# v pooled over four tokens by one load and three adding transfers, with new orders of instructions

## The chip, the cores and the metric

The kernel runs on one core of a Trainium2 chip. The metric is the device time of one execution in microseconds (us). The core has five engines that each take their instructions in order: TensorE (PE) for matmuls and transposes, VectorE (DVE), ScalarE (ACT) and GpSimd (POOL) for work on vectors, SyncE (SP) that here only issues transfers. A transfer (DMA) is issued by an engine and carried out by 16 DMA engines; who needs its data waits for a semaphore that it raises when it has landed.

## The reference

Inputs are q, k and v (4 batches, 8 heads, 576 tokens, 64 numbers each) and five weight arrays. For each batch:

```
q_d, k_d, v_d = means of q, k, v over groups of 4 tokens      # 144 tokens
coarse = softmax(q_d k_d^T / 8) v_d, each row repeated 4 times
local  = softmax(q k^T / 8 over |i - j| < 4) v
x      = coarse + local                                       # 576 x 512, heads side by side
u      = x + Re(fft over tokens and over the 512 features of x)
x      = u + relu(layernorm(u) @ w_ch1) @ w_ch2               # 512 -> 2048 -> 512
gate   = sigmoid(causal convolution of x with 5 taps per feature)
out    = (gate * (x @ w_val)) @ w_out
```

The change concerns v_d, which the coarse attention multiplies from the right.

## The kernel before, in words

Features or keys lie on the 128 partitions, tokens along the free dimension. Large matmuls split each float32 operand in two float16 parts, high and low, and add the products (the tiles hh and hl, u, W, FH and FL). Work comes in 4 batches; the part after the attention runs in 3 units of 192 tokens per batch, 12 in all. Batch 0 has code of its own for its attention (lines 1600 to 1830), which fills the first 60 us or so together with the preparation of the weights; the attention and the transform of batches 1 to 3 are interleaved with the MLP and the gated part of the batch before, whose matmuls (lines 1319, 1340, 1389, 1494, 1510) are the bulk of PE's work.

In batches 1 to 3 the function `dense` makes the list of steps of the local attention and of what it loads, and `lowres` that of the coarse one. The coarse part takes the pooled q and k from a tile qkT, computes the scores of a head on PE (sc, line 957), the exponentials E on ACT, transposes them (eT, line 992; copied to ET by ACT) and multiplies them by the pooled v (po, line 1002). Pooled v is the tile `vr`, 72 partitions (keys) x 2 (halves of the keys) x 512 (heads and numbers), in float32. It is a sum over the four tokens, the division by 4 standing in the copy to ET.

How vr comes about before: v lies in DRAM as `v_p` with the four tokens of a group apart (indices: batch, half of the keys kc, token r of the group, key, head and number). `pool_v4(n)`, n from 0 to 3, loads a quarter of it (half of the keys, four of the eight heads) in two transfers of 72 x 2 x 256 into two tiles v, and `pooled_v` adds them: `ptv` = tokens 0 + 1, `vr` = tokens 2 + 3, `vr` = vr + ptv. GpSimd does all three (the helper `add` with engine G, line 528). So a batch takes 8 loads of 144 KB, issued by SP, and 12 additions by GpSimd; three batches take 24 and 36. The tiles v are in the ring `pr` of two slots, ptv in the ring `E` of three, and vr in the ring `M` of two, which kT (k of the dense part) uses too. Batch 0 makes its pooled v on PE (line 1761) and isn't touched.

The order in which each engine takes its instructions is written out by hand in the table `ORDER`: one text for each engine, of numbers `part.index`, a part being a step of the program and the index the place of an instruction among those that the part gives to that engine. A loop at the end (line 2061) ties the instructions in that order; semaphores for the data come on top. Which slot of a ring a tile takes is written in the table `SLOT`. Nothing moves by itself when a step gets shorter: an engine goes on with the next instruction of its row as soon as that one's waits are met.

Other names that follow: `dP` are the weights of the local attention, scaled by 1/sum on GpSimd for some groups (helper at line 525); `vw` is v by windows for the local attention; `uc` and `sq` are the sums of x over the features and of its squares, for the layernorm; `r` is 1/sqrt of the variance by Newton steps on GpSimd (lines 1178 and 1184), which DVE and then ACT turn into the normalised `u`; `sx` and `sums`/`so` are weights on their way to float16 through DRAM; `fs` a sum for the transform; `s_` and `iv_` are scales (powers of two) and their inverses, from `p2a` and `p2b` (lines 573 to 577).

Of the kernel before, what the change touches and what calls it, by code (L numbers as in the profile page):

```python
# [14 lines left out]
ALU = mybir.AluOpType  # L15
# [5 lines left out]
QC = SD // 2  # L21
# [22 lines left out]
    "prp.E": "0120120101202102120120120120120121021201201201220210210210210210210210120102102102100201201201201201201201210210210",  # L44
# [6 lines left out]
    "prp.pr": "010101010101010101010110101010010101",  # L51
# [15 lines left out]
225.0-2 195.2 237.1 237.0 237.2 238.1 238.0 225.3 238.2 267.1 267.0 275 277 280.1 280.0 282 283.1 283.0 285.0 294.1-3  # L67
291.0-1 294.4 291.2 298.0 291.3-8 326.1 286.0 298.1 298.3 298.2 286.1 285.1 326.0 347.0 121 347.1-3 403.0 333.1 333.0
367.1 367.0 345 367.2 368.0-1 369 368.2 370.1 403.1 433 315 370.0 370.2 403.2-3 408 412 424 419 423 427 444 450.1
450.0 430.1 430.0 499.0 488.1 488.0 467 499.1 488.2 491.1 491.0 492.1 491.2 492.0 492.2 499.2-3 493.1 493.0 493.2  # L70
546.0-1 539 535 546.2-3 545.0 550.1 550.0 545.1 553 554 559.1 559.0 609 639
""",
    "vector": """
0 30 20 18 21 32 25.1 25.0 28 41.1 41.0 48.0 27 38 48.1 23 48.2 54 65.0 31 58.0 34 65.1 42 59 71 77.1 77.0 75 58.1 60
85 55 56 63 68 73 52 81.0 86 81.1-3 140 67 81.4 70.0-1 70.3 70.2 83 130 129 132 107 81.5 109 110 113.1 113.0 114 117
118 125 81.6 79 143 84 169.3 88 136 137 139 133 167.0 145 146 147 150 153 131.0 154 156 157 159 165 163 192.1 167.1
160 169.0 192.0 169.1 169.4 164 167.2 209 168.0-1 131.1 192.2 193.0 168.2 192.3 192.5 192.4 131.2 170.0 169.2 169.5
170.1-2 210 186 187 172.0 197.1 197.0 247.0 171.0 211 171.1-2 172.3 172.1 172.4 212 193.1 172.5 172.2 174.0-1 227
247.1-2 193.2 247.3 174.2 197.2-3 228 197.4 224.0-1 253.0 197.5 173 247.4 229 258 247.5-6 188 259 253.1 239.0 239.3
232 189 239.4 239.1 255.2 230 239.5 239.2 255.0-1 255.3 265 224.2-3 225 234 233 241 249.3 249.0 253.2 269 224.5 224.4  # L80
253.3-5 292.0 236 292.1 274 257.0 257.3 253.6-7 292.2 249.1 249.4 278 243 249.5 249.2 253.8-10 302.0 246 253.11 292.3
257.1-2 261.0 253.12 302.2 253.13 261.1 257.4-5 263.3 263.0 299.0 302.1 253.14 293.0 284 407.0 302.3 251 292.4-5 288
263.1-2 263.4 261.2 303.3 303.1 261.3 263.5 303.2 267.1 304.1 293.1 293.3 304.2-3 300 293.4 303.0 261.5 261.4 293.2
267.0 299.1 305 293.5 295 271.0 310 273.0 271.2 271.1 273.2 273.1 261.6 271.3 314 275.1 299.2 273.3 275.0 323 306.1
296.0 277.1 277.0 275.2 277.2 327 299.3-4 335 296.1 280.0 306.2 280.1 282.0 407.1 296.2 407.2 296.3-4 283.0 304.0
296.5 282.1 283.1 306.3 297.0-1 306.0 309 407.4 285 297.3-5 286 291.0-1 338 291.2 342 297.2 291.3 294.0 291.4 322
326.1 326.0 294.1-2 350.1 313.0 326.2 291.5 339 291.6 326.3 313.1 333.1 333.0 298.0 311.0 354 350.0 298.2 298.1 357
311.1 364 407.3 328.3 328.1 328.0 328.2 329.1-2 329.0 331.2 331.1 329.3 332 334.2 334.1 371 331.3 331.0 334.0 334.3
341.0 319 341.1 379 347.0 324 344 347.1-2 345.0-1 355.0 333.2 356.0 333.3 347.3-4 388 355.2 359.0 462.1 366 355.1
347.5-6 356.2 359.2 347.7 345.2 355.3 356.1 345.3 356.3 347.8 395 376.0 376.3 347.9 400 359.3 359.1 378.0-2 347.10  # L90
361.1 378.3 361.0 406.1 361.3 406.0 378.4 376.1-2 376.4 361.2 413 381.0 372.0 376.5 372.1 410 377.0 387.0 381.3 377.1
387.1-3 414.0-1 462.0 383.0 381.4-5 381.1-2 429 462.2 383.1 387.4 383.2 420 538.0 417.0 414.3 385.0 414.2 385.3 417.3
417.1-2 421.3 393.2 385.1-2 383.3 421.1 421.0 538.1 426.0 385.4-5 394.0-3 383.5 426.3 426.1 390.0 390.3 393.3 394.4
390.1 421.2 445 390.2 426.2 434 390.4-5 432 383.6 393.0 397.0-1 383.4 397.2 403.0 397.3 393.1 399.0 399.2 404.0 399.1
404.2 403.1 404.1 403.2 399.3 448 451 408.1 408.0 404.3 403.3 438 412.0-1 408.2 403.4 412.2 403.5-8 419.0 403.9 419.1
455.0 403.10 397.4 446.0 424.0 423.0 439.0 459 446.1 455.1 538.2 424.1 423.1 457 439.1 402.0-3 427.0 427.2 427.1 402.4
460.2 460.1 465 463.2 460.3 473 427.3 466.2 409.0 430.0 471 430.2 430.1 463.1 409.1 430.3 409.2 452.0 409.3 444.0
463.3 452.1 444.1 409.4 466.3 460.0 452.2 474 442 478 452.3 538.4 452.4 415.0 463.0 415.1-2 466.1 469.3 444.2 452.5
415.3 444.3 452.6 450.1 450.0 452.7 415.4 452.8-10 581 452.11-14 452.17 482 422.0 452.18 452.15 484 422.1-3 469.2
469.1 466.0 469.0 422.4 450.2-3 452.16 476.0 479.0 467.0-1 452.19 441 479.1 476.1 467.2-3 489.1 489.0 497.2 496.0-3  # L100
496.5 496.4 496.6 497.1 502.3 502.0 499.0 443 519 502.4-5 502.1-2 504.2 504.1 499.1 508.0 508.3 509.0 499.2 509.1
497.3 497.0 499.3 508.1-2 504.0 508.4-5 538.3 509.2-3 509.5 511.0 499.4 511.1 504.3 509.6 509.4 513.3 513.0 506.2
# [12 lines left out]
624.5 609.13 609.12 616.3 624.4 624.6 616.2 616.0 629.0-2 629.5 609.14-15 623.0 629.6 629.3-4 639.0 633.1 626.0 637.0
# [369 lines left out]
def attn_moe_kernel(ctx, tc, q_t, k_t, v_p, v_w, w1, w2, w_val, conv_t, w_out, c_feat, c_seq, c_band, c_eye, c_plm, out):  # L485
# [261 lines left out]
    def attn_steps(b):  # L747
# [37 lines left out]
        def dense():  # L785
# [1337 lines left out]
```

## Time and profile before

| | |
|---|---|
| median of 3 runs | 656.34 us (656.07 to 657.16) |
| profiled execution, its own time | 656.75 us |
| its span, first to last instruction | 654.7 us |
| mean granted clock of TensorE | 0.989 |
| busy: PE, DVE, ACT, POOL | 644.5, 527.3, 355.3, 103.5 us |
| busy share of the 16 DMA engines, hardware queue | 39.8% |

The profile was taken of one execution. An engine's busy time counts its work, not the issue of transfers or waits on semaphores. The views used below are the page's totals; windows, that is, busy time in stretches of the span; an engine's waits, with what released it; groups of instructions by line; the timeline, where equal instructions that follow each other are one row with a count (x2) and the time from the first one's start to the last one's end; the issues of DMAs; and the chain of waits, followed back from the last instruction. A buffer's number is left out of its name, so W is any of the weight buffers. A releaser is inferred from semaphores.

### The profile page before, as it was taken

Reading aid. Unit: us, or ns where it says so; the run is one execution under the profiler, and the core shown is the slowest. Engines: PE = TensorE matmul, PEld = TensorE weight load, DVE = VectorE, ACT = ScalarE, POOL = GpSimd, SP = SyncE. Lnnn points to the kernel's source line nnn. Section 1 sums busy time; section 2 is a strip of 40 time slices with the busy share of each in tenths; the row PEclk is TensorE's granted clock in tenths of the full one; section 3 lists DMA queues with packets and bytes.
Section 4 is the critical chain, followed back from the end, with each engine's and each line's share of the span. In section 5 each row is a group of like instructions: output and inputs, shape, how many; then the busy total and the mean of one; then the engine's idle time right before and its main releaser. Section 6 shows DMA issues by size and latency. Waiting matters only on the chain.

```text
span 654.7 us, 20391 instructions
## 1 busy us (share of the span) xinstructions
PE 644.5 (98%) x8626; PEld 574.5 (88%) x8627; DVE 527.3 (81%) x1138; ACT 355.3 (54%) x1057; POOL 103.5 (16%) x162
## 2 busy tenths in 40 slices
PE   9989999999999999999999999999999999999997
PEld 4668899999998887998988888997899989998995
DVE  3999989989988876789999969996778787587554
ACT  2787659788644656677444778644232332414223
POOL 0000121310121703510310153032010100100000
PEclk9959999999999999999999999999999999999999
DMA  9994583023343012332482363352524234343201
GB/s 313 393 339 165 210 309 117 20 85 138 108 126 129 2 37 69 102 115 90 137 288 82 116 215 117 112 177 77 180 85 163 98 112 133 113 146 130 99 3 48
DMA packets 44301, 89.96 MB, mean 137 GB/s; under 512 B 3391, under 2 KB 24895, under 8 KB 43186
## 3 DMA queue, kind: packets, MB, share of 16 engines
q1 hardware_dynamic: 44210, 88.67, 39.8%
q8 instruction: 67, 1.10, 0.7%
q14 instruction: 24, 0.20, 0.1%
HBM read 73.77 MB, written 16.65 MB: 138 GB/s over the span
## 4 chain that ended last, share of the span: by engine, by line
PE 85%; DVE 7%; DMA 3%; ACT 2%; POOL 1%; issue 1%; SPq 0%; ACTq 0%; DVEq 0%; POOLq 0%
PE pc L1389 25%; PE ph L1319 11%; PE ph L1340 8%; PE out L1510 7%; PE val L1494 6%; PE p L1340 6%; DVE W L522 3%; PE ab L1070 2%; PE pc L1294 1%; PE po L1761 1%; PE dO L879 1%; PE po L1604 1%; DMA raw<-in_moe_w_ch_dram 1%; PE st L1154 1%; PE sc L957 1%; PE po L1002 1%
## 5 line engine op out<-in xcount | busy, mean ns | idle before, releaser
L1389 PE MATMUL pc<-hh,W 128*128 128x192 f16 x1232 | 169.8, 246 | 0.0
L1389 PEld LDWEIGHTS <-W 128*128 128x128 f16 x1848 | 152.7, 98 | 4.0 <-issue 1.6
L1389 PE MATMUL pc<-hl,W 128*128 128x192 f16 x616 | 129.3, 246 | 0.0
L1319 PE MATMUL ph<-u,W 128*128 128x192 f16 x960 | 94.5, 246 | 0.6 <-ACT u L1199 0.6
L1319 PEld LDWEIGHTS <-W 128*128 128x128 f16 x960 | 80.2, 98 | 2.8 <-issue 1.4
L1340 PEld LDWEIGHTS <-W 128*128 128x128 f16 x1632 | 79.0, 98 | 2.7 <-issue 0.8
L522 DVE SCALAR_TENSOR_TENSOR W<-X,cw,W 128x192 f32<-128x192 f32 x160 | 62.5, 426 | 9.1 <-ACT W L1457 8.8
L1340 PE MATMUL ph<-u,W 128*128 128x96 f16 x960 | 65.1, 206 | 0.2
L1352 ACT ACTIVATE hh<-r 128x384 f16<-128x384 f32 x48 | 24.3, 519 | 71.9 <-DVE r L528 60.2
L1494 PE MATMUL val<-yy,W 128*128 128x192 f16 x576 | 59.1, 246 | 0.1
L1494 PEld LDWEIGHTS <-W 128*128 128x128 f16 x576 | 47.6, 98 | 2.0 <-issue 0.9
L1340 PE MATMUL p<-u,W 128*128 128x96 f16 x672 | 47.9, 206 | 0.0
L1510 PE MATMUL out<-W,gh 128*128 128x512 f16 x144 | 45.8, 379 | 0.0
L528 DVE TENSOR_TENSOR r<-ph,r 128x384 f32<-128x384 f32 (+1 forms) x48 | 21.8, 454 | 21.0 <-PE ph L1340 19.2
L843 ACT ACTIVATE dP<-dS,dmx 128x64 f32<-128x64 f32 x120 | 36.5, 331 | 0.4
L522 DVE SCALAR_TENSOR_TENSOR hl<-r,hh 128x384 f16<-128x384 f32 x48 | 26.2, 564 | 9.4 <-ACT hh L1352 8.9
L528 DVE TENSOR_TENSOR r<-p,r 128x192 f32<-128x192 f32 (+1 forms) x72 | 28.2, 419 | 5.5 <-PE p L1340 3.1
L1323 ACT ACTIVATE hh<-ph 128x384 f16<-128x384 f32 x40 | 19.4, 490 | 19.5 <-PE ph L1319 17.6
L522 DVE SCALAR_TENSOR_TENSOR W<-W,W 128x1024 int32<-128x1024 int32 x24 | 28.9, 1220 | 0.2
L1510 PE MATMUL out<-W,gl 128*128 128x512 f16 x72 | 27.3, 379 | 0.0
L843 ACT ACTIVATION_READ_ACCUMULATOR dP<-dS,dmx 128x1 f32 x120 | 26.9, 224 | 0.0
L1510 PEld LDWEIGHTS <-gh 128*128 128x128 f16 x144 | 14.1, 98 | 13.6
(308 smaller groups left out, 1429.5 us busy)
## 6 DMA issues: line engine op xcount, KB each, us to landing
W<-sums SPq DMA_DIRECT2D x32, 512.0 KB, 4.4
W<-in_moe_w_ch_dram SPq DMA_DIRECT2D x12, 1024.0 KB, 6.9
sm<-sums SPq DMA_DIRECT2D x16, 512.0 KB, 6.7
out_dram<-osb SPq DMA_DIRECT2D x17, 256.0 KB, 4.1
vw<-in_vw_dram SPq DMA_DIRECT2D x8, 512.0 KB, 4.8
w1f<-W SPq DMA_DIRECT2D x8, 512.0 KB, 3.1
sums<-so SPq DMA_DIRECT2D x16, 256.0 KB, 2.9
v<-in_vp_dram SPq DMA_DIRECT2D x24, 144.0 KB
```

The source lines that it names most:

```text
L522: return eng.scalar_tensor_tensor(out=out, in0=in0, scalar=scalar, in1=in1, op0=op0, op1=op1)
L528: return eng.tensor_tensor(out=out, in0=a, in1=b, op=ALU.add)
L843: A.activation(out=s_[:, z, a], in_=pss[par][:, z, a], func=AF.Exp, scale=SCALE, bias=mx[:, par, z, a:a + 1], accum_out=su[:, par, z, a:a ...
L879: T.matmul(out=pos[x][par * 64:par * 64 + 64, a2, o:o + nq], lhsT=vw[g][row, 2 * z + hf, c:c + D], rhs=pts[z][row, par, a2, hf * 64:hf * 6 ...
L1070: T.matmul(out=ps[0:n, c0:c1], lhsT=d[x][:, c, sd, e, n0:n0 + n], rhs=feat[:, w, c, c0:c1], start=(t == 0), stop=(t == 5),)
L1319: T.matmul(out=ps[:, e], lhsT=w1_ap(pw, kc, 2 * g + e), rhs=uh[px][:, kc, :], start=(t == 0), stop=(t == 11))
L1323: A.activation(out=h_, in_=ps, func=AF.Relu)
L1340: T.matmul(out=out[:, e * HT:e * HT + HT], lhsT=w(pw, kc, e), rhs=b_[x](px, kc), start=(kc, pw, px) == (0, 0, 0), stop=(kc, pw, px) == (1, ...
L1352: A.activation(out=h[0], in_=x, func=AF.Relu)
L1389: T.matmul(out=ps[m // 2][:, m % 2], lhsT=w2_ap(pw, kk, m), rhs=x[px][:, e], start=(kk == 0 and (pw, px) == (0, 0) and m % 2 == 0), stop=( ...
L1494: T.matmul(out=ps[:, e], lhsT=wv_ap(pw, kc, 2 * mh + e), rhs=m_["y"][px][:, kc, :], start=(t == 0), stop=(t == 11))
L1510: T.matmul(out=ps, lhsT=(gh, gl)[px][:, kc, t * 128:(t + 1) * 128], rhs=wo_ap(pw, kc), start=(n == 0), stop=(n == 11))
```

## The change

`pool_v4` gets another meaning. Its argument is now r, one of the four tokens of a group. For r = 0, SP loads a 72 x 2 x 512 slice, 288 KB, straight into vr. For r = 1, 2 and 3, GpSimd issues a transfer of the same shape into the same place, with `accum_op=ALU.add`, which adds to what is there. Each of these has to wait until the one before has landed. `pooled_v` is not called any more; the tiles v and ptv are gone, and with them the slots of ring `pr` in `SLOT` and some of ring `E`. A batch has 1 load and 3 adding transfers in place of 8 loads and 12 additions. Step times and all other code stay; since the parts of the program have other instructions, the numbers in `ORDER` are written anew for all five engines, and other instructions are moved by that too. PE does the same matmuls as before.

```diff
@@ -895,13 +891,15 @@
                 steps.append((0.1, lambda z=z: [load_k(z, 0, KW), load_q(z, 0, S)]))
             steps.append((0.1, lambda: [load_vw(g) for g in range(3)]))
 
-            def pool_v4(n):
-                x = [pr_t("v4", [QC, 512]) for _ in range(2)]
-                kc, h = n // 2, n % 2
-                for r in range(2):
-                    load(out=x[r].rearrange("p (r c) -> p r c", r=2),
-                         in_=v_p[b, kc, 2 * r:2 * r + 2, :, h * 256:h * 256 + 256].rearrange("r g c -> g r c"))
-                pooled_v([(kc, x)], n, h * 4, 4)
+            def pool_v4(r):
+                if r == 0:
+                    new_vr()
+                x = v_p[b, :, r, :, :].rearrange("k g c -> g k c")
+                o = d["vr"].rearrange("p k h d -> p k (h d)")
+                if r == 0:
+                    load(out=o, in_=x)
+                else:
+                    nc.gpsimd.dma_start(out=o, in_=x, accum_op=ALU.add)
             v1 = [(0.1, lambda n=n: pool_v4(n)) for n in range(4)]
             for z in range(2):
                 for w in range(1 if b == 1 else 2):
```

In the tables:

```diff
-    "prp.E": "0120120101202102120120120120120120121021201201201220210210210210210210210120102102102100201201201201201201201210210210",
+    "prp.E": "0120120101200201201201201201210212012012011021021021021021021012010210210211201201201201201201210210210",
...
-    "prp.pr": "010101010101010101010110101010010101",
...
     "gpsimd": """
-0.0 5.1 5.0 136.1 136.0 137.0 139.1 139.0 137.1 183.0-2 195.1 195.0 193.0-1 0.1 294.0 193.2-8 183.3 219.1 219.0 219.2
...
+5.0 0.1 0.0 5.1 136 137 139.1 139.0 219 183 193 237 225.0-1 225.3 225.2 238 267.1 267.0 275 277 315 280 282.1 283.1
```

Code before the changed function has moved up by four lines in the changed file and code behind it by two, so that line 528 is now 524, 1002 now 1000, and 1184 now 1182.

GpSimd's row in the third batch. Before, from the second of two multiplications of dP on, with ten of the batch's twelve additions behind it:

```order
L525 TENSOR_TENSOR dP_3463<-dP_3463,dsu 128x512
L528 TENSOR_TENSOR vr<-vr,ptv 72x256
L528 TENSOR_TENSOR ptv<-v_3855 72x256
L528 TENSOR_TENSOR vr<-v_3856 72x256
L528 TENSOR_TENSOR ptv<-v_3863 72x256
L528 TENSOR_TENSOR vr<-v_3864 72x256
L528 TENSOR_TENSOR vr<-vr,ptv 72x256 x2
L528 TENSOR_TENSOR vr<-v_3872 72x256
L528 TENSOR_TENSOR uc<-uc 128x192
L761 MEMSET X 128x4x4 x2
L528 TENSOR_TENSOR ptv<-v_3871 72x256
L528 TENSOR_TENSOR vr<-vr,ptv 72x256
```

Now, from the first of that pair on:

```order
L521 TENSOR_TENSOR dP_3435<-dP_3435,dsu 128x512
L521 TENSOR_TENSOR dP_3426<-dP_3426,dsu 128x512
L524 TENSOR_TENSOR uc<-X 128x384
L524 TENSOR_TENSOR uc<-uc 128x192
L902 DMA vr<-in_vp_dram 72x2x512 x3
L524 TENSOR_TENSOR sq<-sq 128x384
L524 TENSOR_TENSOR sq<-sq 128x192
```

The pair of dP and the subtractions for uc come ahead of the transfers, which follow each other with nothing between; the additions are gone.

GpSimd's row in the fourth batch. Before, from the first of the two multiplications of dP on:

```order
L525 TENSOR_TENSOR dP_5685<-dP_5685,dsu 128x512
L525 TENSOR_TENSOR dP_5694<-dP_5694,dsu 128x512
L528 TENSOR_TENSOR uc<-uc 128x192
L528 TENSOR_TENSOR vr<-vr,ptv 72x256
L528 TENSOR_TENSOR vr<-v_6214 72x256
L528 TENSOR_TENSOR ptv<-v_6213 72x256
L528 TENSOR_TENSOR vr<-v_6222 72x256
L528 TENSOR_TENSOR vr<-vr,ptv 72x256
L528 TENSOR_TENSOR ptv<-v_6221 72x256
L528 TENSOR_TENSOR vr<-vr,ptv 72x256
L528 TENSOR_TENSOR sq<-sq 128x384
L528 TENSOR_TENSOR sq<-sq 128x192
```

The last three additions of the batch and then uc (128x384) follow there. Now, from the same pair on:

```order
L521 TENSOR_TENSOR dP_5629<-dP_5629,dsu 128x512
L521 TENSOR_TENSOR dP_5638<-dP_5638,dsu 128x512
L902 DMA vr<-in_vp_dram 72x2x512 x2
L524 TENSOR_TENSOR sq<-sq 128x384
L524 TENSOR_TENSOR sq<-sq 128x192
L902 DMA vr<-in_vp_dram 72x2x512
L524 TENSOR_TENSOR uc<-X 128x384
L1042 TENSOR_TENSOR fs<-X 128x577
```

The two squares sq now stand between the second and the third adding transfer, where they stood ahead of the last three additions.

GpSimd's row at the Newton steps for r in the second batch. Before:

```order
L525 TENSOR_TENSOR r_2586<-r_2586,vv 128x192
L573 TENSOR_SCALAR p2a<-f2s_wo 128x1
L1184 TENSOR_SCALAR r_2586<-r_2586 128x192
L525 TENSOR_TENSOR r_2585<-r_2585,r_2586 128x192
L525 TENSOR_TENSOR r_2586<-r_2585 128x192
L525 TENSOR_TENSOR r_2586<-r_2586,vv 128x192
L1184 TENSOR_SCALAR r_2586<-r_2586 128x192
L525 TENSOR_TENSOR r_2585<-r_2585,r_2586 128x192
L525 TENSOR_TENSOR dP_3032<-dP_3032,dsu 128x256
L528 TENSOR_TENSOR X<-X,DS 128x287
```

Now:

```order
L521 TENSOR_TENSOR r_2558<-r_2558,vv 128x192
L569 TENSOR_SCALAR p2a<-f2s_wo 128x1
L1182 TENSOR_SCALAR r_2558<-r_2558 128x192
L521 TENSOR_TENSOR r_2557<-r_2557,r_2558 128x192
L571 TENSOR_SCALAR p2b<-p2a 128x1
L521 TENSOR_TENSOR r_2558<-r_2557 128x192
L521 TENSOR_TENSOR r_2558<-r_2558,vv 128x192
L1182 TENSOR_SCALAR r_2558<-r_2558 128x192
L573 TENSOR_SCALAR s_wo<-p2b 128x1
L521 TENSOR_TENSOR r_2557<-r_2557,r_2558 128x192
L521 TENSOR_TENSOR dP_3004<-dP_3004,dsu 128x256
L521 TENSOR_TENSOR dP_2999<-dP_2999,dsu 128x256
```

`p2b` and `s_wo`, two small operations on one number per partition, stood behind the chain of r and an operation on X; they now stand within the chain.

## Rows read from the trace of the kernel before

**Rows 1.** The page, busy time: engine, us (share of the span) xinstructions

```profile
PE 644.5 (98%) x8626; PEld 574.5 (88%) x8627; DVE 527.3 (81%) x1138; ACT 355.3 (54%) x1057; POOL 103.5 (16%) x162
```

**Rows 2.** Three stretches: window us, length, each engine busy (xcount), PEclk, DMA share, GB/s

```profile
30.00:40.00 10.00, 7.26 (x44) 5.16 (x44) 9.22 (x17) 8.85 (x53) 0.00 (x0) 0.65 0.92 354
40.00:50.00 10.00, 10.00 (x122) 7.05 (x121) 9.39 (x19) 7.54 (x35) 0.00 (x0) 0.67 1.03 351
420.00:640.00 220.00, 219.96 (x3315) 204.93 (x3313) 164.22 (x381) 72.90 (x146) 18.02 (x24) 1.00 0.34 116
```

**Rows 3.** Waits of PE over the span: us in total, times, longest us

```profile
PE po L1604 <- POOL busy L546: 1.0, 1, 1.0
PE eT L1738 <- DVE E L525: 1.0, 1, 1.0
PE dO L879 <- DMA vw<-in_vw_dram: 0.9, 1, 0.9
PE po L1747 <- ACT ET L1741: 0.8, 1, 0.8
PE ph L1319 <- ACT u L1199: 0.6, 1, 0.6
```

**Rows 4.** Groups of POOL: line, operation, shapes xcount, busy us, mean ns, idle before

```profile
L528 POOL TENSOR_TENSOR vr<-vr,ptv 72x256 f32<-72x256 f32 x12 | 10.4, 873 | 0.6
...
L528 POOL TENSOR_TENSOR ptv<-v 72x256 f32<-72x256 f32 x12 | 10.0, 831 | 14.1 <-DVE dsu L847 7.5 <-PE dO L879 6.5
L528 POOL TENSOR_TENSOR vr<-v 72x256 f32<-72x256 f32 x12 | 9.9, 827 | 23.7 <-DMA v<-in_vp_dram 23.5 <-DVE qkT L890 0.3
L528 POOL TENSOR_TENSOR uc<-X 128x384 f32<-128x384 f32 x6 | 7.3, 1225 | 101.0 <-DVE u L1200 98.2 <-PE st L1154 2.7
```

**Rows 5.** Timeline of POOL: start us, us, line, out<-in xcount [idle before <-releaser]

```profile
72.23 0.32 POOL L573 TENSOR_SCALAR p2a<-f2s_w 128x1 f32<-128x1 f32 x1 [5.46 <-ACT p2t L586]
...
127.39 0.19 POOL L577 TENSOR_SCALAR s_w<-p2b 128x1 int32<-128x1 int32 x1
...
265.50 2.04 POOL L525 TENSOR_TENSOR dP<-dP,dsu 128x512 f32<-128x512 f32 x2
...
281.32 0.73 POOL L528 TENSOR_TENSOR vr<-vr,ptv 72x256 f32<-72x256 f32 x1
...
385.39 2.04 POOL L525 TENSOR_TENSOR dP<-dP,dsu 128x512 f32<-128x512 f32 x2
...
395.04 2.26 POOL L528 TENSOR_TENSOR sq<-sq 128x384 f32<-128x384 f32 x2
...
398.74 0.72 POOL L528 TENSOR_TENSOR vr<-vr,ptv 72x256 f32<-72x256 f32 x1
```

**Rows 6.** Timeline of PE: first products with vr in three batches

```profile
144.88 0.71 PE L1002 MATMUL po<-ET,vr 72*64 72x144 f32 x8
...
286.92 0.71 PE L1002 MATMUL po<-ET,vr 72*64 72x144 f32 x8
...
401.72 0.71 PE L1002 MATMUL po<-ET,vr 72*64 72x144 f32 x8
```

**Rows 7.** Timeline of SP's queue: start us, us of the issue, line, out<-in

```profile
267.02 0.43 SPq L531 DMA_DIRECT2D sx<-w1f  x1
...
380.17 0.33 SPq L531 DMA_DIRECT2D v<-in_vp_dram  x1
```

**Rows 8.** The page, DMA issues: engine op xcount, KB each, median us to landing

```profile
out_dram<-osb SPq DMA_DIRECT2D x17, 256.0 KB, 4.1
...
sums<-so SPq DMA_DIRECT2D x16, 256.0 KB, 2.9
```

**Rows 9.** Chain of waits from 360 to 420 us: start us, us, what

```profile
375.81 7.17 DMA vw<-in_vw_dram
```

**Rows 10.** Line 528 on POOL: xcount: ns min/median/max, first and last start us

```profile
L528 POOL TENSOR_TENSOR ptv<-v x12: 718/732/1761, 73.7 to 397.9; 72x256 f32<-72x256 f32 x12
```

**Rows 11.** Line 1184, same columns as rows 10

```profile
L1184 POOL TENSOR_SCALAR r<-r x4: 353/354/1255, 93.0 to 218.9; 128x192 f32<-128x192 f32 x4
```

More of the change, by code (lines that the diff above doesn't have):

```diff
@@ L76 @@
[L76 to L90, printed above, removed]
@@ new lines @@
+326.16 346.17 348.0 348.10-11 348.1 348.18 348.2 311.0 348.19 348.3-5 348.20 348.12 348.21 348.13-14 348.22 348.15
+348.23 313.0-1 348.16-17 313.2-7 311.1-9 313.8-23 311.10-23 333.0-1 333.3 333.2 333.4-10 333.12 333.11 333.13 333.15
+333.14 333.16 333.18 333.17 333.19 333.21 333.20 333.22-33 341.0 354.0 357.0 341.1-12 354.1-23 357.1-17 360.6
+357.18-23 364.0-2 341.13 360.0-3 360.7-9 360.4-5 360.10-11 360.18 360.12 360.19 364.3-23 371.0-11 341.14-19 360.13
+360.20-21 360.14 360.22 360.15-17 360.23 332.0 365.0-3 365.6-8 365.4 365.9-10 365.5 365.12-15 365.11 365.18-19
@@ new lines @@
+341.20-22 371.12-23 365.20 365.16 365.21-23 332.1-11 379 365.17 343.0-3 374.0 388.0-13 341.23 374.6-7 374.1 374.8
+374.2 374.9 374.3 374.10-11 374.4-5 343.6 343.4-5 343.8 343.7 343.9-14 343.16 343.15 343.17-19 374.18 374.12-13
+374.19-21 388.14 374.14-16 374.22-23 382.6 344.0-7 347.0 388.15 374.17 344.8-23 345.1 345.0 345.2-31 345.33 345.32
+395.0-4 388.16-19 382.0-2 382.7-8 382.3 382.9-11 382.4-5 347.1 349.0-1 388.20-23 349.2-3 395.5-7 382.18 382.12
+382.19-20 382.13 353 400.0-1 395.8 349.4-11 400.2-9 395.9-12 358.0 358.4-7 358.1-3 382.14 382.21 382.15-16 382.22-23
@@ new lines @@
+382.17 395.13-23 400.10-21 391.0 391.6-7 391.1-2 391.8 391.3 391.9-10 391.4 391.11 391.18 391.5 391.12 391.19-20
+391.13-16 391.21 391.17 391.22-23 358.10-11 358.14-15 358.18-19 358.8-9 358.12-13 358.16-17 358.20-39 376.1 376.0
+376.2-3 396.6 396.0 396.7-9 396.1-2 396.10-11 396.3-5 396.12-13 396.18-20 396.14-15 396.21 396.16 396.22-23 396.17
+362.0 362.4 362.1 362.5-6 362.2 362.7 362.3 401.0-1 401.6 400.22-23 401.2-3 401.7-8 401.4-5 401.9 401.12 401.10-11
+401.18 401.13 401.19 401.14 401.20-21 401.15 401.22-23 401.16-17 362.8 362.10 362.9 362.12 362.11 362.14 362.13
@@ new lines @@
+531.78-79 531.61-62 531.80-83 531.63-71 523.19-23 526.6-23 542.0 533.6-8 533.0-1 533.9 533.2 533.10 533.3 533.11
+533.18 533.4 533.19 533.5 533.12 533.20-21 533.13-14 533.22 533.15-17 533.23 534.0-3 534.6-8 534.4-5 534.9-11
+534.18-19 534.12-15 534.20-22 542.1-3 542.24 542.4-7 542.25 542.8-11 534.16 534.23 534.17 536.6 536.0 542.26 542.72
+542.48-50 542.73-75 542.12 542.76 542.13 542.51 542.14 542.27 542.15-16 542.52 542.17 542.53-55 542.18 542.77 542.19
+542.28-29 542.20 542.78 542.21-23 542.30-36 542.56 542.37-38 542.79 542.39 542.57 542.40-41 542.58 542.42 542.59
@@ new lines @@
+570.59 570.18 570.79 570.19 570.30-31 570.80-81 570.60 570.82-83 570.32-37 570.20 570.38-41 570.21 570.42-47 570.61
+570.22 570.62 570.23 570.63-66 568.23 568.16-17 570.67-71 571.6-7 571.0-1 571.8 571.2 571.9-10 571.3-5 571.11-12
+571.18 571.13-14 571.19-22 571.15-17 571.23 578.0 572.0 578.1-11 572.1-2 572.6-8 572.3-4 572.9 572.5 572.12-14
+572.10-11 572.15 572.18-19 572.16 572.20-23 572.17 573.0-4 573.6 573.5 573.12 573.7 573.13 573.8-10 573.14 573.11
+573.15-23 594.0 578.48 578.12 578.72 578.13-16 578.49-51 578.73 578.17 578.52 578.18 578.74 578.19-29 578.53-57
@@ new lines @@
+648.21-23 648.16-17 653.12-18 653.24 653.19-20 653.51 653.25 653.21 653.26-30 653.52 653.31-33 653.53 653.34-35
+653.54-56 653.36-40 653.57 653.72 653.58 653.73-75 653.59-61 653.22-23 653.41-46 653.62 653.76 653.63-67 653.47
+653.77-81 653.68-70 653.82 653.71 653.83 652.5-17 649.6-11 649.18-20 649.0 649.21 649.1 649.22 649.2-4 649.23 649.5
+649.12-13 658.72 658.24 658.48 658.0 658.73 658.1-2 658.25 658.3-5 658.26 658.6 658.27 658.7-11 649.14-17 654.0-1
+654.6 654.2-4 654.7-10 654.5 654.11-13 654.18 654.14 654.19 654.15 654.20 654.16 654.21 654.17 654.22-23 652.18-21
@@ L364 @@
+687.19-23 688.0 688.12 688.1-7 688.13 688.8-11 688.14-23 703 701.0-1 704.0 705.0-5 704.1-23 705.6-23 701.2-4 707.0-5
+706 707.6-11
 """,
```

541 lines of the change are left out of this document (260 added, 281 removed), and 6 rows, old and new, of the table ORDER.

## The prediction, made before the changed kernel ran

> **What bounds the kernel now.** I read the busy shares first: TensorE (PE) is busy 98% of the span [rows 1]. The stretches say where the other 2% is not: from 420 to 640 us PE is busy 219.96 of 220 us, while 30 to 40 us holds only 7.26 of 10 [rows 2]. The list of what PE waits for then names the releasers. Its five longest entries are a GpSimd (POOL) memset at the start, an exponential E that VectorE (DVE) scales, a load of vw, a copy ET by ScalarE (ACT) and the normalised input u of ACT, together 4.3 us [rows 3]. So an edit can gain only what PE idles, 654.7 - 644.5 = some 10 us in all, and it can lose without limit, by making PE wait where it now waits for nothing. None of the five entries is an addition of the pooled v.
>
> **What is removed.** The 36 additions of GpSimd are three groups of 12: 9.9 + 10.0 + 10.4 = 30.3 us [rows 4] of the 103.5 that GpSimd is busy [rows 1]. What covers them is that vr is ready before PE wants it. In the third batch the last addition ends at 281.32 + 0.73 = 282.05 and PE's first product with vr starts at 286.92; in the fourth it ends at 398.74 + 0.72 = 399.46 and PE starts at 401.72 [rows 5, 6]. The margins are 4.9 and 2.3 us, so removing the additions pays nothing by itself: 0 us. SyncE (SP) loses 24 issues of v, 0.33 us in the row shown [rows 7], and gains 3; nothing on PE's list waits for an issue: 0 us.
>
> **What is added.** Per batch there is one load into vr and then three transfers that add into the same tile. Each waits until the one before has landed, and GpSimd, which takes its instructions in order, stands still during that wait. Call t the time from one such issue to the landing that releases the next. No row shows a transfer of this kind: it moves 288 KB and must read its destination. The nearest rows are transfers of 256 KB, 2.9 and 4.1 us from issue to landing [rows 8]; the longest is a 512 KB load of vw, 7.17 us [rows 9]. These are the bounds. I take 4.1: the rows nearest in size, at their slower value because of the reading.
>
> Third batch: GpSimd's two dP multiplications end at 265.50 + 2.04 = 267.5 [rows 5], at the latest, since an addition stood ahead of them. Two subtractions for uc follow, the larger 1.2 us on average [rows 4], so GpSimd is free by 270. The load r = 0 stands among loads of sx, of which one was issued at 267.02 [rows 7]; put at 268 with 2.9 for the way, it lands near 271, and this releases the first adding transfer. So vr is done at 271 + 3t, 283.3 at t = 4.1. The new order puts five matmuls more ahead of PE's first product with vr, some 0.4 us where they follow each other; PE wants vr at 287.4. The margin is 4.1 us, and it is gone at t = 5.5.
>
> Fourth batch: the load r = 0 takes the place of a load of v that was issued at 380.17 [rows 7], and has landed by 387.3 even at 7.17. The dP pair ends at 385.39 + 2.04 = 387.4. Then come r = 1, r = 2, the two squares sq (before, from 395.04 to 397.3) and r = 3 [rows 5]. So vr is done at the later of 387.4 + 3t and 397.3 + t; at 4.1 these are 399.7 and 401.4. Thirty matmuls more stand ahead of PE's product, most of them short ones; I put them at 1.3 us, so PE wants vr at 403.0. The margin is 1.6 us, gone at t = 5.2 by the first sum and 5.7 by the second. Queued behind the waiting transfers are sq in the third batch, uc and fs in the fourth. There sq itself needs GpSimd by 395.04, and GpSimd has left the wait for r = 1 at 387.4 + t, in time up to t = 7.6. So at 4.1 both batches cost 0 us.
>
> Second batch: the third adding transfer stands behind the scale of w2, whose last operation before ended at 127.39 + 0.19, and the first product with vr, which was at 144.88 [rows 5, 6], has 38 matmuls fewer ahead, at most 3.2 us. That leaves 14 us for one transfer, or two: 0 us. The first one stands ahead of the scale of w1 and waits for its load; that scale ran at 72.23, after GpSimd had idled 5.46 us [rows 5], so a load that lands up to there costs nothing.
>
> [...] The trace shows GpSimd being held up: the same 72 x 256 addition takes 0.718 us at best and 1.761 at worst [rows 10]. [...]
>
> **What is moved.** The tables of all five engines are new. In the second batch GpSimd's Newton steps for r now have two more small scalar operations among them, 0.19 us each by the row of their kind at 127.39 [rows 5], +0.4 us in front of u, for which PE already waits 0.6 [rows 3]. But one operation of that chain took 1.255 us where its median is 0.354 [rows 11]; if that falls to the median, the whole 0.6 goes. Bounds -0.6 and +0.4; I take 0, between them. The wait for vw (0.9, [rows 3]) stays, since two loads of W still stand ahead of that load and the load of vr only behind it: bounds -0.9 and +0.9, and I take 0. In start-up, loads of W, q, and constants change places. PE works at a mean granted clock of 0.65 and 0.67 from 30 to 50 us [rows 2]. [...] The waits for E (1.0) and ET (0.8) fall in start-up too, where an operation that comes 1 us later in their chain costs 1 us, and more if the slow stretch lasts longer. Bounds: -3, all the waits of start-up (the memset's 1.0 with them), and +3 the other way; no row favours a side, so 0.
>
> Sum: 656.75 (the profiled execution's own time) + 0 = 656.75. That execution lies 0.41 above the median of the runs shown, 656.34, so the forecast is 656.3. The small bounds of the r chain and of vw, with part of those of start-up, give it 655.0 to 657.6.
>
> **Rivals.** *Faster through the new order.* Shorter waits at E, ET, vw and u, and an earlier end of the low clock. For it: 4.3 us of named waits, 2.8 of them in start-up, and a GpSimd freed of 30 us. Against it: GpSimd idles for 5.46 us up to 72.23 [rows 5], so its work doesn't hold up the start, and the late stretches have nothing to give. Half of the waits, 2.1, and 0.5 from the clock make 656.3 - 2.6 = 653.7.
>
> *Slower: PE waits for vr.* Above t = 5.2 PE stands at its first product with vr in the fourth batch, and above 5.5 in the third too. At t = 6.2: 271 + 18.6 - 287.4 = 2.2 and 387.4 + 18.6 - 403.0 = 3.0, so 656.3 + 5.2 = 661.5. At 7.17 it is 5.1 + 5.9 = 11.0, and 667.3. For it: the three are serial, no row bounds the adding part, and GpSimd's operations stretch to 2.4 times. Against it: transfers of this size are at 2.9 to 4.1.
>
> *Slower through start-up.* A load of weights or constants comes late, PE's chain grows by some 1.5 us, and the low clock adds half as much: 656.3 + 2.2 = 658.5. For it: the stretch from 30 to 50 us already runs short of work and clock [rows 2]. Against it: no entry of PE's list there is a load.
>
> **How the numbers follow.** No change 0.40; faster by the order 0.32; slower by vr 0.15; slower by start-up 0.13. About 0.2% (1.3 us) is what a measurement of this kernel can tell from no change. So faster 0.32, same 0.40, slower 0.28. The range 653.4 to 660.5 leaves out the best tenth, in the faster case, and waits for vr beyond t = 6.
>
> **What would show it.** Right: GpSimd's busy time falls by about 30 us, PE's list has no entry for its products with vr (now line 1000), and the stretches after 50 us are as full as before. The step on t is wrong if vr or a transfer releases PE at that line near 287 or 403 us; the step on start-up if the low-clock stretch is longer or shorter by over 1 us; the r chain if u costs PE more than 1.0 us. The forecast is wrong if these sum to more than 1.3 us.

## The result and the profile after

The changed kernel took 662.58 us (median of 4 runs, 661.34 to 666.2), the kernel before 656.55 in the runs beside it (656.07 to 657.16): ratio 1.010, 95% interval 1.0057 to 1.0144. It is slower by 6 us, and 2.1 us outside the range. The profiled execution is the slowest of the four, 666.2 us (span 664.4), so its trace is of the largest loss; the other three lie at 661.3 to 663.6. Its mean granted clock is 0.984, and that of the two fastest 0.990, as in the kernel before (0.989): a loss by the clock is in the profiled execution, and not in those two.

Busy time of the engines in the changed kernel [rows 1]; then its stretches, window us, length, busy time of PE, PEld, DVE, ACT, POOL, granted clock, DMA share, GB/s [rows 2]:

```profile
PE 647.2 (97%) x8626; PEld 577.5 (87%) x8627; DVE 521.9 (79%) x1138; ACT 355.4 (53%) x1057; POOL 83.0 (12%) x135
```

```profile
20.00:30.00 10.00, 9.69 (x93) 7.16 (x89) 9.58 (x22) 6.70 (x32) 0.00 (x0) 1.00 0.80 305
30.00:40.00 10.00, 7.72 (x45) 5.54 (x44) 8.63 (x18) 9.26 (x53) 0.00 (x0) 0.61 1.00 365
40.00:50.00 10.00, 9.86 (x121) 6.69 (x120) 7.46 (x14) 8.56 (x34) 0.00 (x0) 0.71 1.02 363
50.00:60.00 10.00, 8.13 (x90) 6.09 (x89) 9.29 (x16) 5.16 (x11) 0.00 (x0) 0.83 0.69 232
390.00:400.00 10.00, 9.73 (x240) 9.08 (x235) 3.71 (x9) 4.74 (x12) 3.93 (x4) 0.83 0.47 114
420.00:640.00 220.00, 220.00 (x3360) 205.28 (x3359) 164.60 (x393) 75.95 (x164) 18.13 (x24) 1.00 0.35 120
```

Three of these stretches before, which [rows 2] does not show:

```profile
20.00:30.00 10.00, 9.84 (x92) 7.11 (x88) 9.77 (x19) 8.19 (x35) 0.00 (x0) 1.00 1.02 378
50.00:60.00 10.00, 9.79 (x136) 8.17 (x135) 9.21 (x18) 6.86 (x12) 0.00 (x0) 1.00 0.31 120
390.00:400.00 10.00, 10.00 (x163) 7.86 (x163) 9.49 (x17) 8.85 (x26) 7.26 (x10) 1.00 0.52 178
```

GpSimd's busy time fell by 20.5 us, not 30.3: against what was said of busy times ahead of the prediction, the nine issues of adding transfers are counted in it, with 1.1 us each. From 420 us on all is as before. The losses lie in 50 to 60 us, where PE is busy 8.13 of 10 us (9.79 before), between 280 and 420, and with some 1 us between 100 and 280. The lower clock has spread in this execution: 0.83 in 50 to 60 and in 390 to 400, where it was 1.00.

What PE waits for in the changed kernel, the three longest entries [rows 3]:

```profile
PE dO L875 <- DMA vw<-in_vw_dram: 1.9, 1, 1.9
PE mir L1824 <- ACT X L1694: 1.9, 1, 1.9
PE po L1000 <- DMA vr<-in_vp_dram: 1.5, 1, 1.5
```

All three have come or grown: mir, in start-up, from 0.2 to 1.9 us; vr, which was no entry, 1.5; and the vw load, 0.9 to 1.9. They are not all. PE's whole list adds up to 12.7 us, from 5.8 before: 5.9 (3.9 before) up to 60 us, 2.2 (1.0) from there to 270, where a wait of 1.0 for uc of DVE is new, and 4.6 (0.9) from 270 to 420. These 6.9 us more, and 2.7 us more of busy time for the same matmuls at a lower clock, make up 9.6 of the 9.7 us by which the span has grown. The wait for vr is 1.5 of them.

The chain of waits of the changed kernel in the third batch (start us, us, what):

```profile
271.43 4.00 DMA vr<-in_vp_dram
275.43 0.35 issue
275.79 4.92 DMA vr<-in_vp_dram
280.71 0.41 issue
281.12 4.88 DMA vr<-in_vp_dram
286.00 0.40 issue
286.40 6.33 DMA vr<-in_vp_dram
292.73 0.14 issue
292.86 0.71 PE po L1000 x8
```

This is the serial chain that the prediction spelled out: the load of token 0 (4.00 us), then three adding transfers. One takes 4.9 us to land and 0.4 more until the next is issued, so t = 5.3, and the last even 6.3. From 275.43 to 292.73 they need 17.3 us where 3 x 4.1 = 12.3 was put in. This is the third batch. In the fourth the third transfer is issued at 404.65 and PE's first product with vr starts at 412.26; there PE waits 0.6 us for ET, and not for vr.

The wait at mir is followed back on three engines. DVE waits for a load of W; behind its work ACT's square of W waits, which stands ahead of the copy of X in ACT's order; PE's mir needs that copy (start us, us, engine, line, operation [idle before <-releaser]):

```profile
50.68 1.30 DVE L617 TENSOR_SCALAR W<-W 128x1024 int32<-128x1024 int32 x2 [2.33 <-DMA W<-in_moe_w_ch_dram]
...
51.89 3.49 DVE L518 SCALAR_TENSOR_TENSOR W<-W,W 128x1024 int32<-128x1024 int32 x3
```

```profile
53.20 1.06 ACT L670 ACTIVATE Wz<-W 128x1024 bf16<-128x1024 f32 x1 [2.36 <-DVE W L518]
...
54.26 0.97 ACT L1694 ACTIVATE X<-dO 128x456 f32<-128x456 f32 x2
```

```profile
54.84 1.24 PE L1824 MATMUL mir<-X,mirror 128*128 128x289 f32 x4 [1.87 <-ACT X L1694]
```

SP's queue of the changed kernel shows why the load is late, and the same queue before shows where it stood:

```profile
14.12 0.77 SPq L527 DMA_DIRECT2D vw<-in_vw_dram  x1
28.32 0.38 SPq L527 DMA_DIRECT2D X<-in_q_dram  x1
28.74 1.49 SPq L527 DMA_DIRECT2D W<-in_moe_w_ch_dram  x3
30.28 3.98 SPq L1240 DMA_DIRECT2D w1f<-W  x2
34.31 0.43 SPq L527 DMA_DIRECT2D seq<-in_c_seq_dram  x1
34.78 0.44 SPq L527 DMA_DIRECT2D W<-in_moe_w_ch_dram  x1
```

```profile
11.99 0.80 SPq L531 DMA_DIRECT2D W<-in_moe_w_ch_dram  x2
...
16.87 1.02 SPq L531 DMA_DIRECT2D W<-in_moe_w_ch_dram  x2
28.28 0.38 SPq L531 DMA_DIRECT2D X<-in_q_dram  x1
```

Before, four loads of W were issued up to 17.9 us, W9's second among them, ahead of the load of q that SP issues only at 28.3. In the changed row two of the four stand behind that load, and W9's, the last, behind two stores and seq as well: 34.78 in place of about 12.4. SP takes its row in order, so from 14.9 to 28.3 us it issues nothing (17.9 to 28.3 before), and the DMA engines are at a share of 0.80 from 20 to 30 us (1.02 before).

### The profile page after: what moved, and what is told of

Read it like the earlier page. It is cut to its first block, busy times and chain, and to the rows that moved or that the text cites. A ratio compares the mean times of both kernels' runs of the same rounds, so it can differ in the third digit from the quotient of the medians.

```text
span 664.4 us, 20336 instructions
## 1 busy us (share of the span) xinstructions
PE 647.2 (97%) x8626; PEld 577.5 (87%) x8627; DVE 521.9 (79%) x1138; ACT 355.4 (53%) x1057; POOL 83.0 (12%) x135
## 4 chain that ended last, share of the span: by engine, by line
PE 83%; DMA 7%; DVE 3%; ACT 3%; issue 1%; POOL 1%; SPq 1%; DVEq 0%; ACTq 0%
PE pc L1387 23%; PE ph L1317 10%; PE ph L1338 7%; PE out L1508 7%; PE p L1338 6%; PE val L1492 5%; PE pc L1292 3%; PE ph L1281 3%; DMA vr<-in_vp_dram 3%; PE ab L1068 2%; PE dO L875 1%; PE po L1759 1%; DMA vw<-in_vw_dram 1%; DMA raw<-in_moe_w_out_dram 1%; PE st L1152 1%
## 5 line engine op out<-in xcount | busy, mean ns | idle before, releaser
L1492 PE MATMUL val<-yy,W 128*128 128x192 f16 x576 | 57.4, 246 | 0.1
L518 DVE SCALAR_TENSOR_TENSOR hl<-ph,hh 128x384 f16<-128x384 f32 x40 | 21.9, 550 | 8.3 <-ACT hh L1321 8.1
```

The source lines that it names most:

```text
L518: return eng.scalar_tensor_tensor(out=out, in0=in0, scalar=scalar, in1=in1, op0=op0, op1=op1)
L1492: T.matmul(out=ps[:, e], lhsT=wv_ap(pw, kc, 2 * mh + e), rhs=m_["y"][px][:, kc, :], start=(t == 0), stop=(t == 11))
```

## The experiments

Ratios are of a kernel to the kernel before on the same chip, with their 95% intervals; a profiled trace is one execution.

**New pool, old orders.** `pool_v4` of the change in the kernel before, its ORDER otherwise kept:

```diff
 "sync"
-... 199 195.0 204 ... 332 367 368.0 318.1-2 ... 475 491.0 437.2 491.1 505.0 ...
+... 199 195 204 ... 332 367 318.1-2 ... 475 488 437.2 505.0 ...
 "gpsimd"
-... 367.1 367.0 345 367.2 368.0-1 369 368.2 370.1 403.1 433 315 370.0 370.2 403.2-3 ...
+... 345 368 369 370 403.1 433 315 403.2-3 ...
-... 467 499.1 488.2 491.1 491.0 492.1 491.2 492.0 492.2 499.2-3 493.1 493.0 493.2 ...
+... 467 499.1 491 492 499.2-3 493 ...
```

> The orders of the kernel before with only the changed pool_v4 in them. SP's load of token 0 stands where a load of v stood; GpSimd's three adding transfers stand in place of the additions (third batch: behind both dP; fourth: one behind the dP pair, uc, then two, then the squares). Theory A (the transfers cost the time): 660 to 663 us. Theory B (the new orders do, start-up first): start-up as before; at 5.3 us each the transfers end near 285 us in the third batch, in time for 286.9, and near 404 in the fourth, 2 to 3 us late: 658.5 to 660 us.

In the kernel that ran, the third transfer of the fourth batch stands behind the squares (`491 492 499.2-3 493`), as in the changed kernel, and not ahead of them, as the expectation has it. An earlier form, with the load of token 0 of the fourth batch where the first load of v had stood, has no time: in its orders engines wait for each other in a circle.

662.0 us against 656.72: 1.008 (1.0065 to 1.0094). Theory B's 658.5 to 660 fell short: in the old orders the new pool alone costs about as much as the whole change (1.010, 1.0057 to 1.0144). PE's two longest entries, and the chain of that run's fourth batch:

```profile
PE dO L877 <- DMA vw<-in_vw_dram: 2.8, 1, 2.8
PE po L1002 <- DMA vr<-in_vp_dram: 1.5, 1, 1.5
```

```profile
375.87 9.08 DMA vw<-in_vw_dram
...
398.26 2.08 POOL sq L526
400.41 0.53 POOL sq L526
400.94 5.68 DMA vr<-in_vp_dram
...
406.76 0.71 PE po L1002 x8
```

The two squares stand ahead of the third adding transfer and wait for ACT until 398.2, so the transfer starts at 400.94, and PE gets vr at 406.76 (before: 401.72). In the third batch the transfers end in time, as theory B had it: PE's first product with vr starts at 286.92, as before. Up to the issue of the vw load at 375.87 (before: 375.81) this execution has lost nothing; all of its loss arises in the fourth batch and begins with this load, which takes 9.08 us where it took 7.17 [rows 9]. The squares' lateness follows from it: the chain goes from vw over PE's products, DVE and ACT to the squares. No adding transfer is under way when vw takes longer, since the third batch's have landed by 286.9 and the first of the fourth is issued at 387.19. Why it takes longer is not shown.

**Old orders, no adding at all.** The same kernel without the three adding transfers per batch; tokens 1 to 3 are left out.

```diff
-                else:
-                    nc.gpsimd.dma_start(out=o, in_=x, accum_op=ALU.add)
```

> Old orders with one load of token 0 per batch and nothing else: neither the 36 additions nor the nine adding transfers (tokens 1 to 3 are missing in the pooled v). It bounds what the change could have gained at best. If the additions were hidden, as predicted, and the waits of the run with old orders (662.0) all came from the adding transfers: 656 to 657.5 us, no gain. If GpSimd's additions had cost anything: under 655.5. If the 288 KB load alone makes vw late: PE's wait for vw stays near 2 us and the time is 658.

656.01 against 657.13: 0.9979 (0.9964 to 0.9994). So the 36 additions, together with the three quarters of v's bytes that this run does not load, were worth 0.2%, 1.4 us (0.4 to 2.4), and no more could be had. PE's entry at dO here:

```profile
PE dO L877 <- ACT dP L841: 0.7, 1, 0.7
```

The 288 KB load alone does not make vw late: at dO, PE waits for ACT, not for vw. Set against the run above, the nine adding transfers cost 1.008 - 0.998 = 1.0%, about 6.6 us (with the two intervals, some 1.4 us either way), in the old orders.

**New orders, no adding.** The same two lines taken out of the changed kernel.

> The changed kernel without its nine adding transfers (tokens 1 to 3 of each group are left out of the pooled v); the load of token 0 and all orders stay. Theory A: 656 to 658 us, PE waits nowhere for vr, and the vw load near 381 us takes about 7.2 us as before, not 8.4. Theory B: 659.5 to 661.5 us, with the wait of PE at mir near 53 us (2 us) still there.

660.39 against 657.11: 1.0042 (1.0026 to 1.0058), as theory B had it. Measured from the run with old orders and no adding, the new orders cost 1.0042 - 0.9979 = 0.6%, 4 us, some 1.4 either way; the adding transfers, 1.010 - 1.004, take another 0.6% there, but with the wide interval of the changed kernel (0.4% either way) this is only just clear of nothing. So both theories hold a part. The sum of the two, 6.6 + 4, is larger than the 8 us that the changed kernel lies above the run without either; that the parts overlap is not shown by these runs, whose intervals are as wide as the difference, but by a pair further below: with the new orders and W9's load early, adding costs 1.0086 - 1.0046 = 0.4%, less than the 1.0% of the old orders by more than the intervals.

**New orders, old additions.** The eight loads and twelve additions per batch written back into the changed kernel, their orders set by hand.

```diff
 "gpsimd"  -139.0 219 183 193 237 ... 345.0 403.0-1 368 369 370 ... 467 491 492 499.2-3 493
           +139.0 183 195 193 219 ... 345.0 403.0 367 368 369 370 403.1 ... 467 488 491 492 499.2-3 493
```

> The orders of the changed kernel, with the old eight loads and twelve additions per batch put into them. Theory A: the transfers are gone, so the time goes back to 656 to 658 us. Theory B: start-up and the waits for uc, vw and u stay, and only the wait for vr at 291 us (1.6) goes: 660 to 662 us.

683.08 against 657.11: 1.0392 (1.0372 to 1.0412), which neither theory expected. The mixture has a wait of its own:

```profile
PE dPT L860 <- DVE dP L523: 10.2, 1, 10.2
```

PE stands once for 10.2 us, for a dP of DVE, a wait that neither kernel has. So the run does not answer the question; what additions cost in the new orders stays open. PE's wait at mir is on its list with 1.6, so that this wait does not need the transfers.

**Copying in place of adding.** `accum_op` left out, so that a transfer overwrites; only the last token counts.

```diff
-                    nc.gpsimd.dma_start(out=o, in_=x, accum_op=ALU.add)
+                    nc.gpsimd.dma_start(out=o, in_=x)
```

> The changed kernel with the nine GpSimd transfers copying instead of adding (the last token's copy stands as the pooled v). If reading and adding is what makes a transfer take 5.3 us from issue to the next issue, they fall to about 4, the time of SP's load of the same 288 KB; if it is GpSimd's way of issuing them, they stay at 5.0 to 5.4.

From issue to landing 4.2 us where adding takes 5.0 (medians of nine), and GpSimd's issues follow each other at 4.3 us. GpSimd's row in its third batch, the copies, and the last two adding transfers of the changed kernel for comparison:

```profile
274.51 0.76 POOL L902 DMA_DIRECT2D vr<-in_vp_dram  x1 [4.77 <-DMA vr<-in_vp_dram]
278.84 0.71 POOL L902 DMA_DIRECT2D vr<-in_vp_dram  x1 [3.56 <-DMA vr<-in_vp_dram]
283.07 0.70 POOL L902 DMA_DIRECT2D vr<-in_vp_dram  x1 [3.52 <-DMA vr<-in_vp_dram]
```

```profile
281.12 1.12 POOL L902 DMA_DIRECT2D vr<-in_vp_dram  x1 [4.15 <-DMA vr<-in_vp_dram]
286.40 1.13 POOL L902 DMA_DIRECT2D vr<-in_vp_dram  x1 [4.17 <-DMA vr<-in_vp_dram]
```

An issue takes 0.7 and 1.1 us. So adding costs 1.0 us per transfer from issue to issue; whether the 0.4 us of the longer issue are a part of it is not shown. Without it PE has no wait for vr. The one run took 661.65 us; a single run can't say how much of the loss is left.

**Halves.** Each adding transfer cut by kc, each half waiting for its own predecessor.

```diff
-                    nc.gpsimd.dma_start(out=o, in_=x, accum_op=ALU.add)
+                    for kc in range(2):
+                        nc.gpsimd.dma_start(out=o[:, kc], in_=x[:, kc], accum_op=ALU.add)
```

> The changed kernel with each adding transfer cut in two of 144 KB, each half waiting only for the same half of the token before. If a transfer's time is mostly fixed, a half takes nearly as long as the whole (4 to 4.5 of 5.0 us) and a round of two still some 5 us; if it is mostly bytes, a half lands in 2.5 to 3.5 us and a round takes 3.5 to 4.5, so that PE no longer waits for vr in the third batch.

A half lands in 4.3 us (median of 18), the whole in 5.0, as the expectation had it for mostly fixed time. But the round went as it had it for mostly bytes: the two halves overlap, so that a token takes 3.75 us (issues of the first halves of the three tokens in the third batch at 274.06, 277.78 and 281.56) in place of 5.3, and PE's wait for vr is gone. How much of a transfer's time is fixed is not settled, since each half had the other beside it. The one run took 663.61 us, with the waits for vw (2.0) and mir (1.2) still there, so a gain on 662.58 is not shown.

**The load of W9 early.** In the changed kernel one number of SP's order:

```diff
-... 16.1 185.0 123.1 15.1 15.0 15.5 199 201 16.2 15.2 122.1
+... 16.1 185.0 15.2 123.1 15.1 15.0 15.5 199 201 16.2 122.1
```

> The changed kernel with one edit in SP's order: the load of the last of w_ch1's tiles (W9 in the code) is issued ahead of the load of q that keeps SP waiting until 28.3 us, and no longer at 34.8 us. If this load holds up start-up (DVE waits 2.3 us for it near 50 us, ACT's square of W then stands ahead of the copy of X, and PE waits 1.9 us at mir), all three waits shrink to under 0.5 us and the time falls by 2 to 3 us, to 658.5 to 660.5. If DVE's or ACT's own new order is the cause, nothing moves: 661.5 to 663.

> Both edits: W9's load early, and the nine adding transfers left out (tokens 1 to 3 are missing in the pooled v). If the two causes are separate they add up: 660.4 of the run without adding, less 2, makes 658 to 658.7; what then remains over 656.5 (some 1.5 to 2 us) belongs to other moved instructions, uc and u of the second batch, the vw load and the end of the fourth batch. If nothing else was made worse: 656.5.

With the adding: 661.71, 1.0086 (1.0068 to 1.0103). Without it: 659.09 against 656.72, 1.0046 (1.0026 to 1.0066). The waits did vanish. DVE takes the same operations of W at once, 2.9 us earlier, and mir is on neither list (this row: no adding):

```profile
47.77 1.29 DVE L617 TENSOR_SCALAR W<-W 128x1024 int32<-128x1024 int32 x2
```

But the times hardly followed. By the medians each lies 1 us nearer to before than its partner (6.0 to 5.0 and 3.3 to 2.4 us above it); by the ratios one pair falls (1.010 to 1.0086) and the other rises (1.0042 to 1.0046), both well inside the intervals. A gain is not shown, and the 2 to 3 us expected were not had. What remains, 2.4 us by the medians, is in the trace without adding at several places: the vw load (1.4, from 0.9 before), uc (0.8, new), u (0.8, from 0.6), a copy FH (0.8, new). These were not tried one by one.

**The kernel before with W9's load late.** The mirror of it:

```diff
-... 15.3 15.2 119.3 195.1 15.1 15.0 123.1 123.0 15.4 16.2 122.0
+... 15.3 119.3 195.1 15.1 15.0 123.1 123.0 15.4 16.2 15.2 122.0
```

> The kernel before with the load of W9 moved behind that of seq, as in the changed kernel (issued near 35 us in place of 12.8). If this load alone makes start-up late: +1.5 to +3 us, 658 to 659.5, with a wait of DVE for W near 50 us. If the wait needs the changed orders of DVE and ACT as well: within 1 us of before.

668.24 against 656.72: 1.0182 (1.0166 to 1.0199), 11.5 us, far more than expected. In the old order of DVE an operation on W9 stands ahead of E:

```profile
46.01 0.69 DVE L621 TENSOR_SCALAR W<-W 128x1024 int32<-128x1024 int32 x1 [11.60 <-DMA W<-in_moe_w_ch_dram]
...
47.02 0.75 DVE L525 TENSOR_TENSOR E<-E,lsu 72x576 f32<-72x576 f32 x1
```

DVE waits 11.6 us for the load, and PE 12.2 us for E. So one load issued 23 us later (35.65 in place of about 12.4) can cost 11.5 us; the new orders of DVE had moved W9's operations back, and with these PE waits only some 2 us there.

**The second batch alone.** Old orders; the load and adding transfers in batch 2, additions in batches 3 and 4. The line that picks between the two (`pool_v4a` is the changed function):

```diff
-            v1 = [(0.1, lambda n=n: pool_v4(n)) for n in range(4)]
+            v1 = [(0.1, lambda n=n: (pool_v4a if b == 1 else pool_v4)(n)) for n in range(4)]
```

> The orders of the kernel before; the load and adding transfers in the second batch alone, where PE has 14 us to spare, the old loads and additions in the third and fourth. Theory C (a transfer costs only where PE waits for vr, or for a load beside it): no loss, 656 to 657 us. If the missing additions also shorten the chain of the normalisation between 70 and 230 us, where the run with old orders had gained 1 us on before by 230 us: 655.5. Theory A (a transfer costs wherever it is): a third of 5.3 us, 658 to 658.5.

659.21 against 657.69: 1.0028 (1.0012 to 1.0044). So the place with 14 us to spare also loses, 1.8 us by the ratio (0.8 to 2.9). That is the third of 5.3 that theory A gave, but not its mechanism: the loss does not lie where the transfers are. They are issued between 97.4 and 132.9 us, vr is no entry of PE's list, and the vw load of the fourth batch is issued at 375.36, 0.45 us earlier than before. What grows stands behind that, where nothing was changed:

```profile
PE dO L879 <- DMA vw<-in_vw_dram: 1.8, 1, 1.8
PE eT L1001 <- ACT osb L1537: 0.8, 1, 0.8
```

The first was 0.9, the second is new. This is one execution, and the cause is not settled; but as in the run with old orders above, the loss begins at the vw load (8.03 us here) with no adding transfer under way.

**vr's load behind vw, transfers ahead of the squares.** Old orders, two moves in the fourth batch; and the first move alone in the changed kernel with W9 early:

```diff
 "sync"    -437.1 475 488 437.2               "gpsimd"  -467 499.1 491 492 499.2-3 493
           +437.1 475 437.2 488                         +467 491 499.1 492 493 499.2-3
```

> Old orders with the changed pool_v4 in all three batches, as the run with old orders, with two moves in the fourth batch: SP issues the load of vr behind the second load of vw and no longer ahead of it, and GpSimd issues all three adding transfers ahead of the two squares. If the 288 KB load beside vw made vw late (9.1 us, PE waited 2.8), and the squares held back the last transfer, PE's wait for vw falls to about 1 us and that for vr to under 1: 658 to 660 us in place of 662.0. If vw is late for another reason: 661.5 to 663.

> The changed kernel with W9's load early, as before, and SP's load of vr in the fourth batch behind the second load of vw. Against 661.7 with the early load alone: if the load of vr delays vw, PE's wait for vw falls from 2.1 to about 1.2 us, and the time to 660 to 661; if not, 661.5 to 662, or more where vr itself then comes too late.

The first took 667.34, 1.0144 (1.0123 to 1.0166): worse by 0.6% than without the moves. PE's list and GpSimd's row:

```profile
PE st L1154 <- POOL sq L526: 3.8, 1, 3.8
PE dO L877 <- DMA vw<-in_vw_dram: 1.7, 1, 1.7
```

```profile
396.17 1.14 POOL L904 DMA_DIRECT2D vr<-in_vp_dram  x1 [5.99 <-DMA vr<-in_vp_dram]
401.52 1.12 POOL L904 DMA_DIRECT2D vr<-in_vp_dram  x1 [4.21 <-DMA vr<-in_vp_dram]
402.25 2.09 POOL L526 TENSOR_TENSOR sq<-sq 128x384 f32<-128x384 f32 x2
```

The squares wait on GpSimd behind the third transfer's wait and start at 402.25 (395.04 before), and PE waits 3.8 us for them; vr is no entry. With vr's load behind it, PE's wait for vw is 1.7, from 2.8, and not the 1 that was expected if that load alone delayed it. The second took 662.24 against 657.69, 1.0087 (1.0066 to 1.0108), no better than the early load alone. vw's wait fell from 2.1 to 1.6 in the traces, and vr's in the third batch is still there with 0.9, from 1.4.

## Why the prediction was wrong

- *"So at 4.1 both batches cost 0 us"*: the step that failed first. Its term t was mis-sized. It was 5.3, and 6.3 for a last one. The rows taken were of SP's transfers, which neither add nor are issued by GpSimd. Copying from GpSimd takes 4.3 from issue to issue, adding 1.0 more. The bounds, 2.9 to 7.17, held it. With the measured 16.9 us for three the prediction's own sum for the third batch ends at 271 + 16.9 = 287.9, 0.5 behind its 287.4; PE waited 1.5. That this comes out so near has some luck in it, for both ends stand later in the trace: the load of token 0 was issued at 271.43 and not 268, and took 4.00 and not 2.9, and PE came for vr at 291.4, since it had lost about 4 us by then. In the fourth batch, where the margin was thought to be the smaller, the changed kernel has no wait for vr. What stretches an addition of GpSimd from 0.718 to 1.761 us [rows 10] no run shows.
- *"the later of 387.4 + 3t and 397.3 + t"*: the 397.3, the end of the squares in the trace of before, did not hold. That GpSimd is back in time for the squares did: they wait 4.4 us for ACT in the changed kernel, 4.3 in the run with old orders, and not for a transfer. But ACT is late. In the run with old orders the squares end at 400.9, the third transfer starts only then, and with 5.68 to land PE gets vr 5.0 us later than before. The runs with old orders, with and without adding, differ by 6.6 us, more than the 1.5 us that PE's list names at vr: the longer vw load (9.08 us where before had 7.17), and 0.91 as mean granted clock from 380 to 400 us, after PE has stood 2.8 us for vw, where before and the run without adding have 1.00, are the rest of what the traces show there.
- *Start-up, "no row favours a side, so 0"*: failed too. It was bounded by -3 and +3 but not read. The place of the load of q in SP's row, and what stands behind it, is in the orders; the time at which SP can issue it is in the trace of before (28.28). Together they say that two loads of W move from 17 to 29 us and one from 12.4 to 35. PE's wait at mir grew by 1.7 us. Read in stretches of 1 us from 30 to 62 us, the granted clock of the two profiled executions is 1.00 or 0.50, but for the stretches in which it goes from one to the other (0.97 and 0.71 before; 0.58, 0.59, 0.53 and 0.77 in the changed kernel). With these divided between the two, an estimate, 0.50 lasted 13.6 us before, from 32.9 to 46.6, and 17.1 us in the changed kernel, from 32.2 to 45.8 and from 56.1 to 59.5. The rival "slower through start-up" describes just this, a load of weights that comes late, with 2.2 us; it had 0.13. The prediction's terms for the clock in its rivals, 0.5 us in one and half of 1.5 in another, are estimates that no run shows. With W9's load put back the wait at mir is gone, but a gain in time is not shown, and 0.67% (1.0046 against 0.9979) remains between the new orders and the old ones without adding. So this load is not what the new orders' 4 us rest on; their cause stays open.
- *The additions removed, 0 us*: nearly. They were worth 0.2%, at the edge of what can be told.
- *The r chain, 0*: right within bounds; PE's wait for u is 0.8, from 0.6.
- *The vw load, 0 between -0.9 and +0.9*: +1.0. It took 8.40 us. Why is not settled: in the new orders it took 8.4 and 8.6 with adding transfers and 7.9 and 8.0 without; in the old ones 9.1 with them, 8.0 with those of the second batch alone, and 7.2 before, one execution each, and none with an adding transfer under way.
- *uc*: the prediction's list of what is moved has no term for it. PE waits 1.0 us for uc of DVE between 130 and 270 us, in the run with new orders and no adding too.

The rival "PE waits for vr", at 661.5, has the transfers as the cause, and leaving them out confirms that; but the wait it names is 1.5 us of the loss, and its 3.0 us in the fourth batch did not come in the changed kernel. That its time lies 1 us from the measured one is luck. Its t of 6.2 for all three transfers is a value that no run shows; in the third batch they took 5.3, 5.3 and 6.3 us. The third rival had start-up. The loss of 6 us is some of both and of waits that neither names. They were given 0.28 together, and each was priced alone, as if the other did not happen.

## What to carry to other kernels

Replacing hidden work by a chain of transfers that wait for each other makes its latency the thing to size: three waits of 5.3 us on an engine that takes its row in order are 16 us in which work queued behind them can be late, as the squares were with all three transfers ahead of them, while the additions had let other work in between. A loss also need not lie where the change is: with the transfers in the second batch alone it lay in the fourth, and a time that a theory forecasts, as the third of 5.3 there, does not yet show its mechanism. Where instructions are moved on the engine that issues loads, look first for the instruction in its row that waits longest, and list which loads have passed from ahead of it to behind it. And price rivals that can happen together as a sum.

## What the runs showed of the hardware

A transfer that adds into SBUF took 4.8 to 7.5 us, median 5.0, for 288 KB from issue to landing in the changed kernel (up to 8.8, median 5.2, with the old orders), and 1.1 us of GpSimd for the issue; a copy of the same size and issuer 4.2 and 0.7; adding 144 KB, two at a time, 4.3 and 0.9.
